# A spectral mix and a gated ReLU feed-forward on one core: the first pair's weights in a layout of their own, and v + g·z made ready in the second sequence round

## The chip, the cores and the metric

The kernel runs on one core of a Trainium2 chip. The metric is the device time of one execution in microseconds (us). The engines are TensorE (PE, matrix multiplication), VectorE (DVE, element-wise work from SBUF and PSUM), ScalarE (ACT, activations and casts), GpSimd (POOL) and SyncE (SP). Here POOL and SP only start transfers between the memory (HBM) and the on-chip memory (SBUF).

## The reference

With x of 2048 x 512, weights of 512 x 1792 (gate, up) and 1792 x 512 (down), and real and imaginary DFT matrices:

```python
g = _sigmoid((x * gate_w).sum(-1, keepdims=True))
a = x @ dft_hid_re.T ;  b = x @ dft_hid_im.T
y = dft_seq_re @ a - dft_seq_im @ b
v = (relu(x @ W_gate) * (x @ W_up)) @ W_down
return g * y + (1 - g) * v
```

(the einsums written as products). The result is v + g·(y − v).

## The kernel before

**Arithmetic.** Every float32 operand is split into a high part (a cast to the PE's float32 format, `h`) and a low part (the rest, `l`). A product is three matmuls: high·low, low·high and high·high (`PARTS`). The casts are made on ACT (`scalar.copy`), the low parts on DVE (`tensor_sub`). Around this lies a scheme of seven block products in place of eight (`LEFT`, `RIGHT`, `ORDER`), so many sums of blocks go through DVE. A matmul is 128 x 128 against 128 x 512.

**Stages, in PE's order.**

1. A warm-up of eight matmuls on a constant tile (`warm_up`).
2. The first pair of hidden blocks for the first half of the tokens, without the seven-product scheme (`Direct`, 96 matmuls). It uses the raw slots of the weights `w0` in the layout of all others, four slots by two halves of d. Slots 1 and 3 are loaded first, then 0 and 2, each as a strided load.
3. The other pairs (`Block`), gate and up, with ReLU and the product h = relu(gate)·up. h and its sums go to the memory (`hd`).
4. The DFT along the hidden axis (`SpectralBlock`), stored as `ad`, and the two last pairs.
5. Two rounds with the down weights (`Down`). They read `hd`, and write v to `vd` and −v to `zd`.
6. Four rounds of the DFT along the sequence (`Sequence(left, m, p)`), 336 matmuls or 76.2 us each. m is 0 for the real part, 1 for the imaginary part, p is the half of the columns of tokens. Their order is (0, 0), (0, 1), (1, 1), (1, 0). The rounds with m = 0 accumulate their result into `zd` by DMA, so that `zd` holds the real part of y minus v. The rounds with m = 1 take `zd` up, multiply by the gate g, add v and store `out`. So out = v + g·(z of this round + zd).

In a round the products come in the order 1, 3, 5, 7, 6, 2, 4. Blocks 12 and 22 are complete after product 6 (`done`), block 11 after product 2 (`middle`) and block 21 after product 4 (`end`). The DFT matrix is loaded as `r11`, `r22`, `r12`, `r21`, four tiles of each per round (`rights`), summed on DVE (`r<-r,r`), cast on ACT (`ch`) and split on DVE (`cl`). The left operands of the rounds with m = 1 are loaded from `lb` during the second round.

**What sets the order.** A planner in Python (`Plan`) collects every operation with a key, which is the place in PE's order near which it is wanted. `due` (lines 178 to 187) gives each a due time from its users, `order` (189 to 252) makes a list schedule with modelled times, a pool of 51 tiles in SBUF (4 KB for each partition) and eight PSUM banks. PE keeps program order, DVE and ACT take what is ready among the next 48 by due time, SP and POOL take transfers in the order of the plan. The chip then runs each engine's list in order, with semaphores. A load's place in SP's list is therefore fixed, and it waits for the tile it goes into to be free. Every instruction is issued in `Step.run`, so all have line L123 in the profile, and operations are told apart by their tiles.

**The places that the change touches.** `Step` and `Plan` (costs and due times), `x_load` (372), `Weights.load` (412), `block` (449), `Direct` (540 to 579), `Sequence` (847 to 920), `warm_up` (927) and the opening loads behind it, the loop over the rounds (1052 to 1057), and the layout of the inputs on the host (1093 to 1103). The opening loads, which SP issues in this order:

```python
(w0.load, 0, (1, 4, 2)), (x_load, 0, "11", (0, 1)), (x_load, 0, "11", (1, 2)), (w0.load, 1, (1, 4, 2)),
(x_load, 0, "21"), (lambda: load(gwt[:], gw),), (w0.load, 0, (0, 4, 2)), (w0.load, 1, (0, 4, 2)),
(w1.load, 0), (x_load, 0, "12"), (x_load, 0, "22"), (w1.load, 1)
```

Of the kernel before, what the change touches and what calls it, by code (L numbers as in the profile page):

```python
# [89 lines left out]
class Step:  # L90


    def __init__(self, key, engine, name, a, k):
# [13 lines left out]
        if name == "dma_start":  # L107
# [18 lines left out]
class Plan:  # L126
# [5 lines left out]


# [44 lines left out]
    def due(self):  # L178

        last, n = {}, self.now  # L180
        for s in reversed(self.steps):
            if s.engine == "tensor" and s.key >= 0:
                n -= 1
            mine = n if s.engine == "tensor" else s.key + self.REST
            s.due = min(mine * self.MATMUL, last.get(s, 1e9) - s.work - (self.LANDING if s.name == "dma_start" else 0))
            for x in s.after:
                last[x] = min(last.get(x, 1e9), s.due - self.WAIT)

    def order(self):
# [12 lines left out]
        while any(todo.values()):  # L202
            best = None
            for e, queue in todo.items():
                found = None
                for s in queue[:1 if e == "tensor" else 48]:
# [31 lines left out]
            if s.name == "dma_start":  # L238
                free[s.engine] = t + (0.9 if s.engine == "gpsimd" else 0.06)
# [39 lines left out]
def kernel(ctx: ExitStack, tc, xP, xG, wgu, wd, cr, ci, wri, gw, out):  # L279
# [77 lines left out]

    def store(o, i):
# [13 lines left out]
    def x_load(q, b, ks=(0, 2)):  # L372
        k, j = int(b[0]) - 1, int(b[1]) - 1
        ks = slice(*ks)
        load(piece[q, b][:, ks], xP[2 * q + j, k, :, ks])
# [28 lines left out]
    class Weights:  # L404
# [7 lines left out]
        def load(self, i, s=(0, 4, 1)):  # L412
            s = slice(*s)
            load(self.raw[i][:, s], wgu[self.c, i, :, s])
# [33 lines left out]

    def block(w, i, s):
        s = slice(s, 4, 2)  # L450
        E().scalar.copy(w.b[i][0][:, s], w.raw[i][:, s])
        E().vector.tensor_sub(w.b[i][1][:, s], w.raw[i][:, s], f32(w.b[i][0][:, s]))
# [87 lines left out]
    class Direct:  # L540
        def __init__(self, w):
            self.w, self.x = w, {b: [buf(f"xb{b}{x}", dtype=F32R) for x in "hl"] for b in ("11", "21", "12", "22")}
# [3 lines left out]
            for j in range(2):  # L546
                for d in range(2):
                    for i in range(2):
                        for f in range(2):
                            pe(6, self.product, d, f, i, j)  # L550
                            if d == 1:
                                op(plan.now, self.evac, f, i, j)
            h_out(0, w.c, self.h, plan.now + 200)

        def x_hi(self, b, ks=(0, 2)):
            ks = slice(*ks)
            E().scalar.copy(self.x[b][0][:, ks], piece[0, b][:, ks])

        def x_lo(self, b, ks=(0, 2)):
            ks = slice(*ks)  # L560
            E().vector.tensor_sub(self.x[b][1][:, ks], piece[0, b][:, ks], f32(self.x[b][0][:, ks]))

        def product(self, d, f, i, j):
            ps = self.ps[f, j]
            if d == 0 and i == 0:
                ps.new()
            x = self.x["12"[d] + "12"[j]]
            s = {(1, 1): 0, (0, 0): 1, (0, 1): 2, (1, 0): 3}[f, d]
            for k in range(2):
                for n, (a, b) in enumerate(reversed(PARTS)):  # L570
                    mm(ps[i], self.w.b[i][a][:, s, k], x[b][:, k], start=d == 0 and k == 0 and n == 0,
                       stop=d == 1 and k == 1 and n == 2)
# [274 lines left out]
    class Sequence(Round):  # L847
        HI, LO = 31, 24

        def __init__(self, left, m, p, last=False):  # L850
            self.m, self.p, self.last = m, p, last
# [19 lines left out]
        def gate(self, b):  # L871
            return self.g[:, int(b[1]) - 1].unsqueeze(1).to_broadcast([P, 2, N])

        def done(self, b, key):
# [7 lines left out]
            key += 42 if self.last else 62  # L882
            op(key, lambda: E().vector.tensor_mul(o.all, o.all, self.gate(b)))
            op(key + 2, lambda: E().vector.tensor_add(o.all, o.all, v.all))
            op(key + 8, lambda: load(out[self.place(b)], o.all))

        def middle(self, key):
            if not self.last:
                return super().middle(key)
            z, v = buf("z"), buf("v")  # L890
            op(key - 60, lambda: load(z.all, zd[self.place("11")]))
            op(key - 60, lambda: load(v.all, vd[self.place("11")]))

            def go():
                self.both(E().vector.tensor_add, z, self.ps["A"], z)
                E().vector.tensor_mul(z.all, z.all, self.gate("11"))
                E().vector.tensor_add(v.all, v.all, z.all)
                load(out[self.place("11")], v.all)
            op(key + 14, go)

        def end(self, key):
            if not self.last:
                return super().end(key)

            z, v, o = buf("z"), buf("v"), self.o["21"]
            t, _, es = self.place("21")
            op(key - 90, lambda: load(z.all, zd[t, :, es]))
            op(key - 90, lambda: load(v.all, vd[t, :, es]))

            def ahead():  # L910
                E().vector.tensor_sub(z.all, z.all, self.u2.all)
                E().vector.tensor_mul(z.all, z.all, self.gate("21"))
                E().vector.tensor_add(v.all, v.all, z.all)
            op(key - 32, ahead)
            for n in range(2):
                def go(n=n):
                    E().vector.tensor_mul(o[:, n], self.ps["D"][n], self.g[:, 0])
                    E().vector.tensor_sub(v[:, n], v[:, n], o[:, n])
                    load(out[t, :, es.start + n], v[:, n])
                op(key - 6 + 6 * n, go)  # L920
# [15 lines left out]
    w0, w1 = Weights(0), Weights(1)  # L936
# [3 lines left out]
    for f, *a in (  # L940
            (w0.load, 0, (1, 4, 2)), (x_load, 0, "11", (0, 1)), (x_load, 0, "11", (1, 2)), (w0.load, 1, (1, 4, 2)),
            (x_load, 0, "21"), (lambda: load(gwt[:], gw),), (w0.load, 0, (0, 4, 2)), (w0.load, 1, (0, 4, 2)),
            (w1.load, 0), (x_load, 0, "12"), (x_load, 0, "22"), (w1.load, 1)):
        op(-99, f, *a)
    direct = Direct(w0)
# [3 lines left out]
    op(-90, block, w0, 0, 1)  # L949
    for k in range(2):  # L950
        op(-90, direct.x_hi, "11", (k, k + 1))
        op(-90, direct.x_lo, "11", (k, k + 1))
    op(-90, block, w0, 1, 1)
    op(-90, direct.x_hi, "21")
    op(-90, direct.x_lo, "21")
    op(-90, block, w0, 0, 0)
    op(-90, block, w0, 1, 0)
    op(-90, w1.a_sum, 0)
    op(-90, w1.b_sum, 0)
    op(-90, direct.x_hi, "12")  # L960
    op(-90, w1.a_lo, 0)
# [149 lines left out]
```

## Time and profile before

| what | value |
|---|---|
| median of 3 runs | 798.02 us (798.01 to 798.16) |
| the profiled execution | 798.82 us, span 797.0 us |
| PE busy | 788.4 us (99%), 3464 matmuls |
| weight loads (PEld, beside PE) | 650.9 us (82%) |
| DVE busy | 660.3 us (83%), 784 instructions |
| ACT busy | 330.8 us (42%) |
| POOL busy | 89.4 us (11%) |
| moved by DMA | 188.07 MB, 236 GB/s over the span |

A row of the timeline gives the start in us, the duration, the engine, the operation, the tile written `<-` the tiles read, and how many instructions the row joins. In brackets stands the idle time of the engine before it and what ended it. `xb11h` is the high part of x's block 11, `wb0l` the low part of the first weight tile, `wr` the raw weights. The start of one matmul to the start of the next is shorter than its duration, since they are pipelined. The windows give for each stretch the busy time of every engine with its count of instructions, the granted clock of TensorE, the busy share of the 16 DMA engines and the GB/s. The view of waits names the tile whose writer ended an idle time of PE.

### The profile page before, as it was taken

The numbers are of one execution on the slowest core, as the hardware profiler recorded it, in microseconds if no ns is written. First come the engines' busy times: TensorE is split into PE (matmuls) and PEld (weight loads), VectorE is DVE, ScalarE is ACT, GpSimd is POOL, SyncE is SP. The second block draws the span as 40 slices with busy tenths as digits, with TensorE's granted clock in tenths as the row PEclk, the third lists the DMA queues.
The fourth block names the chain that finished last, engine by engine and source line by source line (L and its number), as shares of the span: only waits on it lengthen the run. The fifth ranks groups of instructions, "written<-read, shape, count | busy, mean of one in ns | idle before, by whom it ended". The sixth has DMA issues, their size and how long they took to land.

```text
span 797.0 us, 9541 instructions
## 1 busy us (share of the span) xinstructions
PE 788.4 (99%) x3464; PEld 650.9 (82%) x3464; DVE 660.3 (83%) x784; ACT 330.8 (42%) x394; POOL 89.4 (11%) x142
## 2 busy tenths in 40 slices
PE   8999999999999999999999999999999999999997
PEld 6888888888888888888888888888888888888885
DVE  6999977768699566899896799997697559977998
ACT  6533222212133134274666668463344235433440
POOL 0101311111112113111121001001000100010000
PEclk9999999999999999999999999999999999999999
DMA  8614553232547599999899989217877994198435
GB/s 321 246 41 145 179 205 146 92 146 93 197 146 228 203 341 417 409 357 330 298 369 415 408 301 346 103 54 196 286 275 272 273 382 135 42 278 314 177 114 158
DMA packets 54111, 188.07 MB, mean 236 GB/s; under 512 B 6192, under 2 KB 7216, under 8 KB 54064
## 3 DMA queue, kind: packets, MB, share of 16 engines
q1 hardware_dynamic: 35344, 119.30, 41.7%
q0 software_dynamic: 18720, 68.17, 24.5%
q8 instruction: 27, 0.44, 0.2%
q14 instruction: 20, 0.16, 0.1%
HBM read 118.23 MB, written 69.21 MB: 235 GB/s over the span
## 4 chain that ended last, share of the span: by engine, by line
PE 84%; DVE 7%; DMA 4%; issue 2%; ACT 1%; SPq 0%; POOLq 0%; ACTq 0%; POOL 0%; DVEq 0%
PE z L123 42%; PE c L123 32%; PE a L123 10%; DVE cl L123 2%; DVE z L123 2%; DVE r L123 2%; DMA r<-ci 2%; DMA z<-zd 1%; DMA wr<-wgu 1%; ACT ch L123 1%; SPq L123 0%; DVE v L123 0%; DVE w L123 0%; DVE xs L123 0%; DVE xb12l L123 0%
## 5 line engine op out<-in xcount | busy, mean ns | idle before, releaser
L123 ACT CAST ch<-r 128x1024 fp32r<-128x1024 f32 x112 | 115.8, 1052 | 131.1 <-PE z L123 53.3
L123 PE MATMUL z<-ch,ll 128*128 128x512 f32 x420 | 163.4, 389 | 0.0
L123 PE MATMUL z<-cl,lh 128*128 128x512 f32 x420 | 163.4, 389 | 0.0
L123 PE MATMUL z<-ch,lh 128*128 128x512 f32 x420 | 163.4, 389 | 0.0
L123 DVE TENSOR_TENSOR cl<-r,ch 128x1024 fp32r<-128x1024 f32 x112 | 134.5, 1220 | 29.1 <-ACT ch L123 22.9
L123 PE MATMUL z<-ch,lb 128*128 128x512 f32 x448 | 137.9, 389 | 0.0
L123 PEld LDWEIGHTS z<-ch,lb 128*128 128x128 f32 x448 | 84.1, 188 | 17.4
L123 PEld LDWEIGHTS z<-ch,lh 128*128 128x128 f32 x420 | 78.8, 188 | 16.5
L123 PEld LDWEIGHTS z<-cl,lh 128*128 128x128 f32 x420 | 78.8, 188 | 16.4
L123 PEld LDWEIGHTS z<-ch,ll 128*128 128x128 f32 x420 | 78.8, 188 | 16.2
L123 PE MATMUL z<-cl,lb 128*128 128x512 f32 x224 | 87.1, 389 | 0.0
L123 DVE TENSOR_TENSOR r<-r,r 128x1024 f32<-128x1024 f32 x64 | 76.4, 1218 | 3.5 <-DMA r<-cr 2.3
L123 DVE TENSOR_TENSOR cl<-hr,ch 128x1024 fp32r<-128x1024 f32 (+1 forms) x56 | 59.9, 1086 | 14.2 <-ACT ch L123 14.0
L123 ACT CAST ch<-hr 128x1024 fp32r<-128x1024 f32 (+1 forms) x56 | 51.8, 942 | 27.1 <-DMA hr<-hd 14.8
L123 PEld LDWEIGHTS z<-cl,lb 128*128 128x128 f32 x224 | 42.0, 188 | 8.8
L123 ACT ACTIVATE g<-c 128x512 f32<-128x512 f32 x26 | 15.6, 598 | 63.7 <-PE c L123 63.5
L123 PE MATMUL c<-xh,wb0l 128*128 128x512 f32 x104 | 40.5, 389 | 0.0
L123 PE MATMUL c<-xl,wb0h 128*128 128x512 f32 x104 | 40.5, 389 | 0.0
L123 PE MATMUL c<-xh,wb0h 128*128 128x512 f32 x104 | 40.5, 389 | 0.0
L123 PE MATMUL c<-xh,wb1l 128*128 128x512 f32 x104 | 40.5, 389 | 0.0
L123 PE MATMUL c<-xl,wb1h 128*128 128x512 f32 x104 | 40.5, 389 | 0.0
L123 PE MATMUL c<-xh,wb1h 128*128 128x512 f32 x104 | 40.5, 389 | 0.0
(210 smaller groups left out, 1318.6 us busy)
## 6 DMA issues: line engine op xcount, KB each, us to landing
hr<-hd SPq DMA_DIRECT2D x42, 512.0 KB, 7.1
r<-cr SPq DMA_DIRECT2D x32, 512.0 KB, 4.9
r<-ci SPq DMA_DIRECT2D x32, 512.0 KB, 11.9
hd<-hs POOLq DMA_DIRECT2D x28, 512.0 KB, 4.6
lb<-lb SPq DMA_DIRECT2D x28, 512.0 KB, 4.7
ad<-a POOLq DMA_DIRECT2D x16, 512.0 KB, 5.9
l<-ad SPq DMA_DIRECT2D x16, 512.0 KB, 8.6
wr<-wgu SPq DMA_DIRECT2D x14, 512.0 KB, 6.4
```

The source lines that it names most:

```text
L123: getattr(getattr(nc, self.engine), self.name)(*map(ap, self.a), **{k: ap(x) for k, x in self.k.items()})
```

## The change

Three things are changed.

*The first pair.* Its weights come as an input of their own, `wf`, with d outermost: for each of two tiles of d, 128 partitions by two halves k by four column groups. A half is one load of 256 KB, 2 KB in one piece for each partition. SP issues the four halves, and ACT's queue issues the four halves of x's blocks 11 and 21 (`side`). The weights `w0` are then loaded in the shared layout only for the later stage. The 48 products for the first tokens run with d, k and the part n outermost, so that four matmuls follow on one part; the high half of x11 is cast on DVE, the others on ACT. The warm-up tile is filled by one memset without a cast. The loads of x12 and x22 come ahead of those of `w1`, and `gwt` last; the sums of `w1` and x get keys in place of a written order.

*The planner.* It gets a cost for `tensor_copy`, 0.5 us for the issue of a transfer in place of 0.06, another rule for due times, and beside the next 48 operations the oldest one as a candidate.

*The last rounds.* The last round's class is now `Last`. Its `prepare` puts work into the second round: the gate row, loads of the four blocks of `zd` and `vd` for p = 0, v + g·z on DVE (8 operations), and four stores into `vd` from POOL. In the last round z of this round is multiplied by g, and v comes as an accumulating transfer (blocks 12 and 22) or as a load, with the sum made by halves (blocks 11 and 21).

```diff
+        if name == "tensor_copy":
+            self.work = 0.1 + n * 0.52e-3
+            self.hold = self.work - 0.05
...
+    ISSUE = {"sync": 0.5, "scalar": 0.5, "gpsimd": 0.9}
...
-            mine = n if s.engine == "tensor" else s.key + self.REST
-            s.due = min(mine * self.MATMUL, last.get(s, 1e9) - s.work - (self.LANDING if s.name == "dma_start" else 0))
+            if s.engine == "tensor":
+                last[s] = min(last.get(s, 1e9), n * self.MATMUL)
+            elif s not in last or s.key > 0:
+                last[s] = min(last.get(s, 1e9), (s.key + self.REST) * self.MATMUL)
+            s.due = last[s] - (s.work + self.LANDING if s.name == "dma_start" else 0)
             for x in s.after:
-                last[x] = min(last.get(x, 1e9), s.due - self.WAIT)
+                last[x] = min(last.get(x, 1e9), s.due - self.WAIT - (x.work if x.name != "dma_start" else 0))
...
-                for s in queue[:1 if e == "tensor" else 48]:
+                near = queue[:1] if e == "tensor" or not queue else [*queue[:48], min(queue, key=turn.get)]
+                for s in near:
...
-                free[s.engine] = t + (0.9 if s.engine == "gpsimd" else 0.06)
+                free[s.engine] = t + self.ISSUE[s.engine]
...
+    def side(o, i):
+        plan.scalar.dma_start(o, i)
...
+            for d in range(2):
+                for k in range(2):
+                    for n in range(3):
+                        for i in range(2):
+                            pe(2, self.products, [(d, i, f, 0, k, n) for f in range(2)])
...
+        def w_split(self, d, k=slice(0, 2)):
+            hi, lo = self.w[d]
+            E().scalar.copy(hi[:, k], self.raw[d][:, k])
+            E().vector.tensor_sub(lo[:, k], self.raw[d][:, k], f32(hi[:, k]))
+
+        def x_split(self, b, k=slice(0, 2), hi=None):
+            x, raw = self.x[b], piece[0, b]
+            (hi or E().scalar.copy)(x[0][:, k], raw[:, k])
+            E().vector.tensor_sub(x[1][:, k], raw[:, k], f32(x[0][:, k]))
...
+    class Last(Sequence):
+        def prepare(self, key):
+            g = gate_row(self.p, key - 60)
+            for i, b in enumerate(BLOCKS):
+                k, z, v = key + 24 * i, buf("z"), buf("v")
+                op(k - 50, lambda b=b, z=z: load(z.all, zd[self.place(b)]))
+                op(k - 50, lambda b=b, v=v: load(v.all, vd[self.place(b)]))
+                op(k, lambda b=b, z=z: E().vector.tensor_mul(z.all, z.all, self.gate(b, g)))
+                op(k + 2, lambda v=v, z=z: combine(v.all, v.all, z.all, 1))
+                op(k + 10, lambda b=b, v=v: store(vd[self.place(b)], v.all))
+
+        def done(self, b, key):
+            o = self.o[b]
             op(key, lambda: E().vector.tensor_mul(o.all, o.all, self.gate(b)))
-            op(key + 2, lambda: E().vector.tensor_add(o.all, o.all, v.all))
-            op(key + 8, lambda: load(out[self.place(b)], o.all))
+            op(key + 4, lambda: accumulate(o.all, vd[self.place(b)]))
+            op(key + 30, lambda: load(out[self.place(b)], o.all))
+
+        def part(self, v, b, n, p, sign):
+            E().vector.tensor_mul(self.o[b][:, n], p[n], self.g[:, 0])
+            combine(v[:, n], v[:, n], self.o[b][:, n], sign)
...
-            z, v, o = buf("z"), buf("v"), self.o["21"]
+            v = buf("v")
             t, _, es = self.place("21")
-            op(key - 90, lambda: load(z.all, zd[t, :, es]))
-            op(key - 90, lambda: load(v.all, vd[t, :, es]))
...
-    ones, warm, wp = buf("ones", [N]), buf("warm", [N], F32R), Pair("warm")
+    warm, wp = buf("warm", [N], F32R), Pair("warm")
 
     def warm_up():
-        E().vector.memset(ones.all, 1.0)
+        E().vector.memset(f32(warm.all), 1.0)
         E().vector.memset(gs.all, 0.0)
-        E().vector.tensor_copy(warm.all, ones.all)
...
+    for d, b in ((0, "11"), (1, "21")):
+        for k in halves:
+            op(-99, direct.w_load, d, k)
+            op(-99, x_load, 0, b, k, side)
+    for f, *a in ((x_load, 0, "12"), (x_load, 0, "22"), (w1.load, 0), (w1.load, 1), (lambda: load(gwt[:], gw),)):
+        op(-98, f, *a)
...
+    for d, b in ((0, "11"), (1, "21")):
+        for k in halves:
+            op(-90, direct.x_split, b, k, plan.vector.tensor_copy if d == 0 else None)
+            op(-90, direct.w_split, d, k)
...
         if n == 1:
+            start = plan.now
...
-        Sequence(lefts[m], m, p, n == 3)
+        if n < 3:
+            Sequence(lefts[m], m, p)
+        else:
+            Last(lefts[m], m, p).prepare(start + 150)
...
+    first = wgu[0][:, :, [[1, 3], [2, 0]]].transpose(2, 1, 4, 0, 3, 5).reshape(2, P, 2, 4, P)
```

More of the change, by code (lines that the diff above doesn't have):

```diff
@@ L278, with kernel @@
 @with_exitstack
-def kernel(ctx: ExitStack, tc, xP, xG, wgu, wd, cr, ci, wri, gw, out):
+def kernel(ctx: ExitStack, tc, xP, xG, wf, wgu, wd, cr, ci, wri, gw, out):
     nc = tc.nc
@@ L559, in x_lo @@
[L559 to L572, printed above, removed]
+            for d in range(2):
[3 more added lines that the diff above has]
+                            pe(2, self.products, [(d, i, f, 0, k, n) for f in range(2)])
+                            if d == k == 1 and n == 2:
+                                for f in range(2):
+                                    op(plan.now, self.evac, f, i, 0)
@@ L881, in done @@
             op(key + 20, lambda: load(v.all, vd[self.place(b)]))
-            key += 42 if self.last else 62
-            op(key, lambda: E().vector.tensor_mul(o.all, o.all, self.gate(b)))
-            op(key + 2, lambda: E().vector.tensor_add(o.all, o.all, v.all))
-            op(key + 8, lambda: load(out[self.place(b)], o.all))
-        def middle(self, key):
[L888 to L899, printed above, removed]
+            op(key + 62, lambda: E().vector.tensor_mul(o.all, o.all, self.gate(b)))
@@ L914, in end @@
-            op(key - 32, ahead)
+                E().vector.tensor_mul(self.u2.all, self.u2.all, self.gate("21"))
+                combine(v.all, v.all, self.u2.all, -1)
+            op(key - 90, lambda: load(v.all, vd[self.place("21")]))
+            op(key - 40, ahead)
             for n in range(2):
[L916 to L920, printed above, removed]
+                op(key - 6 + 6 * n, self.part, v, "21", n, self.ps["D"], -1)
+                op(key - 6 + 6 * n, lambda n=n: load(out[t, :, es.start + n], v[:, n]))
@@ L1096 @@
         "xG": laid(x.reshape(NT, KD, P, D).transpose(0, 2, 1, 3)),
-        "wgu": laid(np.stack([blocks(wg), blocks(wu)], axis=1)),
+        "wf": laid(first),
+        "wgu": laid(wgu),
         "wd": laid(halves(wd)),
```

117 lines of the change are left out of this document (48 added, 69 removed).

## The prediction, made before the result was known

> **What bounds the kernel now.** I read the page's first part, then what TensorE (PE) waited for, then the span cut where PE's work changes character, then the single instructions at both ends.
>
> ```profile
> PE 788.4 (99%) x3464; PEld 650.9 (82%) x3464; DVE 660.3 (83%) x784; ACT 330.8 (42%) x394; POOL 89.4 (11%) x142
> ```
> ```profile
> PE warm L123 <- DVE warm L123: 1.9, 1, 1.9
> PE c L123 <- DVE xb11l L123: 0.5, 2, 0.2
> PE c L123 <- DVE xb12l L123: 0.3, 1, 0.3
> PE c L123 <- ACT xb11h L123: 0.3, 1, 0.3
> ```
> ```profile
> 0.00:5.49 5.49, 3.57 (x8) 2.51 (x8) 1.66 (x5) 2.52 (x3) 0.20 (x4) 1.00 0.51 156
> 5.49:18.79 13.30, 12.27 (x50) 9.04 (x50) 10.54 (x15) 8.45 (x11) 1.28 (x2) 1.00 1.02 381
> 18.79:791.40 772.61, 772.55 (x3407) 639.37 (x3407) 646.10 (x763) 319.83 (x381) 87.95 (x136) 1.00 0.66 234
> 791.40:797.00 5.60, 0.00 (x0) 0.00 (x0) 2.00 (x4) 0.00 (x0) 0.00 (x0) 0.71 0.48 187
> ```
>
> PE is busy 99% of the span, and its list of waits has nothing but the first stage. From 18.79 to 791.40 us it is idle 0.06 us in all. So nothing can be won between these times unless matmuls go, and none goes. What can be won lies before 18.79 and behind PE's last matmul; what can be lost lies anywhere. The rate is 772.61 / 3407 = 0.2268 us per matmul.
>
> The sum is made against the profiled execution, 798.82 us (a span of 797.0 and 1.8 around it). The median of the runs shown is 798.02, 0.8 lower; I carry the difference over. About 0.2%, or 1.6 us, is what a measurement of this kernel can tell from no change.
>
> **The front.** The window 5.49 to 18.79 holds 49 products besides the last warm-up matmul. At 0.2268 each they need 11.11 us and take 13.30: 2.19 us are lost there.
>
> ```profile
> 1.92 3.64 PE L123 MATMUL warm<-warm 128*128 128x512 f32 x8 [1.92 <-DVE warm L123]
> 5.49 0.49 PE L123 MATMUL c<-xb11h,wb0h 128*128 128x512 f32 x1
> 6.22 0.50 PE L123 MATMUL c<-xb11l,wb0h 128*128 128x512 f32 x1 [0.23 <-DVE xb11l L123]
> 18.79 0.50 PE L123 MATMUL c<-xb12l,wb0h 128*128 128x512 f32 x1 [0.32 <-DVE xb12l L123]
> ```
> ```profile
> 0.73 1.28 ACT L123 ACT_TABLE_LOAD   x1 [0.73 <-PEq L1104]
> 3.92 0.62 ACT L123 CAST wb0h<-wr 128x512 fp32r<-128x512 f32 x1 [1.90 <-DMA wr<-wgu]
> 4.82 0.62 ACT L123 CAST xb11h<-x 128x512 fp32r<-128x512 f32 x1 [0.29 <-DMA x<-xP]
> 6.54 0.62 ACT L123 CAST xb11h<-x 128x512 fp32r<-128x512 f32 x1 [1.10 <-DMA x<-xP]
> 7.90 0.62 ACT L123 CAST wb1h<-wr 128x512 fp32r<-128x512 f32 x1 [0.74 <-DMA wr<-wgu]
> ```
> ```profile
> 1.43 0.43 DVE L123 CAST warm<-ones 128x512 fp32r<-128x512 f32 x1
> 5.47 0.69 DVE L123 TENSOR_TENSOR xb11l<-x,xb11h 128x512 fp32r<-128x512 f32 x1 [0.21 <-ACT xb11h L123]
> ```
> ```profile
> 0.74 0.66 SPq L123 DMA_DIRECT2D wr<-wgu  x1
> ```
> ```profile
> GB/s 0 0 0 0 51 322 395 272 221 234 223 211 227 250 311 367 402 371 344 389 422 444 418 401 401 434 401 418 418 401 401 434 401 410 401 410 418 401 401 434
> ```
>
> The pieces of 256 KB set the pace: ACT's casts start as they land, at 3.92 (weights), 4.82 and 6.54 (the halves of x) and 7.90 (weights). In slices of 0.5 us the DMA rate falls from 395 to 211-234 GB/s between 3.5 and 7 us, while the odd slots of w0 move in pieces of 1 KB, and later stands above 400.
>
> *First product.* The new weights come in halves of 2 KB pieces, so the two first pieces (512 KB) should move at about 400 GB/s rather than 220: before, 520 KB had moved by 4.0 and the second piece was in use at 4.82. I put the landing at 4.5, between 3.9 (where the first piece alone was in use) and 5.3 (both late by the lag of the second). ACT now issues four loads first, four times up to 0.66 as on SP from 0.73, then loads its table, 1.28: free at up to 4.65. Its cast takes 0.62, hand-over 0.05. First product: 5.3 to 5.4; I take 5.4. Below, the warm-up sets the end: without the CAST it begins 0.43 earlier and ends near 5.06. Above, 6.0.
>
> *The 49 products.* x11's high part is now a cast on DVE (0.43, as the CAST row) beside ACT's cast of the weights, and four products share each part. For a landing L, DVE does x high to L+0.43, x low (0.69) to about L+1.1, weights low to L+1.75; PE wants them at L+1.6 and L+2.5. The second half is wanted at L+3.4; before, the fourth piece was in use 3.08 behind the second, and 0.62 for its cast makes L+3.7. So 0.15 is lost there (0 to 0.9), where the waits of 0.2 to 0.3 in PE's list, each with a slow restart behind it (6.22 is 0.73 behind 5.49), made most of the 2.19. The warm-up's eight matmuls take 3.64, 0.45 each, half the later rate; up to four first products could run so if the change of rate is late: 4 x 0.2 = 0.8 at most, I take 0.2. x12 comes before the c=1 weights now, so the wait at 18.79 (0.32 by its row) goes. Losses 0.35 instead of 2.19.
>
> The Trainium skill (TensorE: Matmul & The Clock Gate, What's actually happening) says that the array runs at half rate until one busy window of about 3.4 us, which is free-running. The trace agrees for this start (the warm-up is slow from 1.92 to 5.49, 3.6 us); by that rule the 0.2 can be anything up to the 0.8.
>
> The front thus ends (5.49 - 5.4) + (2.19 - 0.35) = 1.9 us earlier. All behind it follows, PE in the same order. The planner's new costs move little on the other engines; the nearest place is a block in which DVE now makes three additions of hs ahead of a product h<-g,c that PE's bank waits for.
>
> ```profile
> 346.15 0.68 DVE L123 TENSOR_TENSOR h<-g,c 128x512 f32<-128x512 f32 x1
> 346.74 0.69 DVE L123 TENSOR_TENSOR hs<-h 128x512 f32<-128x512 f32 x1
> 349.18 0.39 PE L123 MATMUL c<-xh,wb1l 128*128 128x512 f32 x1
> ```
>
> The evacuation ends at 346.83, PE uses the bank at 349.18: 2.35 us of slack, of which three additions, 0.61 from one start to the next, take 1.8. I cost this at nothing; without that cover it would be 1.8.
>
> **The tail.**
>
> ```profile
> 790.95 0.39 PE L123 MATMUL z<-ch,lb 128*128 128x512 f32 x1
> 791.45 0.69 DVE L123 TENSOR_TENSOR v<-v,z 128x512 f32<-128x512 f32 x1
> 792.06 0.68 DVE L123 TENSOR_TENSOR z<-z,gg 128x512 f32<-128x512 f32 x1
> 792.77 0.69 DVE L123 TENSOR_TENSOR v<-v,z 128x512 f32<-128x512 f32 x1
> 792.17 1.66 SPq L123 DMA_DIRECT2D out<-v  x2
> ```
>
> The last matmul ends at 791.34; the last multiplication starts only at 792.06 because DVE is still at the subtraction of the half before it (791.45). In the new order the additions of v for blocks 12 and 22 are gone from DVE (POOL adds by DMA, earlier), so DVE is idle when each half of the last product comes: the first half's pair fits into the time of the second half's matmuls, the last multiplication starts at 791.37. 792.06 - 791.37 = 0.69 off; the subtraction (0.69), its store's issue and landing follow unchanged.
>
> **The second round.** Here the new work goes: 1 gate row, 4 loads of z, 4 of v, 8 DVE operations, 4 stores on POOL.
>
> ```profile
> 581.00:602.00 21.00, 21.00 (x94) 17.38 (x94) 19.15 (x18) 10.48 (x12) 0.00 (x0) 1.00 0.84 300
> 602.00:622.00 20.00, 20.00 (x90) 16.57 (x89) 14.75 (x16) 7.29 (x7) 0.00 (x0) 1.00 0.74 252
> 622.00:640.00 18.00, 18.00 (x82) 14.88 (x81) 8.94 (x9) 5.18 (x6) 2.55 (x3) 1.00 0.99 277
> 640.00:659.00 19.00, 19.00 (x85) 15.76 (x84) 10.68 (x10) 6.86 (x8) 0.84 (x1) 1.00 0.96 359
> ```
> ```profile
> lb<-lb SPq DMA_DIRECT2D x16, 512.0 KB, 4.1
> GB/s 233 198 229 254 323 267 259 272 259 254 285 263 280 272 272 272 280 375 410 427 418 418 418 427 414 414 405 293 276 272 267 418 414 418 418 423 418 194 17 267
> r<-ci SPq DMA_DIRECT2D x10, 512.0 KB, 12.7
> ```
> ```profile
> 657.24 2.35 DVE L123 TENSOR_TENSOR r<-r,r 128x1024 f32<-128x1024 f32 x2
> 659.66 2.36 DVE L123 TENSOR_TENSOR cl<-r,ch 128x1024 fp32r<-128x1024 f32 x2
> ```
> ```profile
> 663.56 0.39 PE L123 MATMUL z<-cl,lb 128*128 128x512 f32 x1
> ```
>
> DVE: 8 operations of 1.18 (the pair at 657.24), 9.4 us, against 41 - 33.9 = 7.1 us idle from 581 to 622. DVE works several us ahead of PE there and is idle for about half of 622 to 659, so they delay its later work by 2.3 and stop nothing; without that lead it would be the 2.3. The first of them waits for the gate row and for z, which SP issues near 581 and 584, 4.1 us before they land as the loads there do; DVE comes to it near 591, and what is queued behind it, the low parts for the next product, is wanted at 598. POOL is idle from 581 to 622, so its four stores hold up nothing.
>
> DMA: 13 transfers of 512 KB are 6.8 MB; at the 414-418 GB/s of full slices, 16.4 us. By bytes, 581 to 622 moved 6.3 + 5.0 = 11.3 MB of a possible 17.0: 13.7 us are spare. By the busy shares only 0.16 x 21 + 0.26 x 20 = 8.6. So 2.7 to 7.8 us are still queued at 622. From there to 659 the queues are full (0.99, 0.96) and take up 0.9 more; the third round's loads, which wait 12.7 us from issue to landing already, land 1.8 to 6.9 later. The nearest need: r's sum at 657.24, the low part at 659.66 (one of the two, ends 660.88), its product at 663.56: 2.68 us of slack. Stall: 0 to 4.2. Full slices move at the high rate, so the count by bytes is nearer; I take a delay of 3.2 and a stall of 0.5. In the last round two z and two v loads go, which can't move PE: it has no wait there.
>
> **Sum**: -1.9 - 0.7 + 0.5 = -2.1. Profiled execution 796.7, median 795.9.
>
> **The rivals.** *(B) The front's gain stays out.* ACT's issues and table load last to 4.65, and both queues share the same engines; if the pieces land as they did (4.82, 7.90), first product 5.5, restart 0.9, half rate 0.8: losses 1.7, front -0.5, sum -0.7, median 797.3. For it: the slices up to 3.5 us show that the first bytes come no earlier than 2 us. Against: the 220 GB/s belong to the 1 KB pieces. The Trainium skill (DMA: Bandwidth & Descriptors, Issuing engines are not separate DMA queues) says that loads started on different engines interleave on the same 16 engines and save only issue time. No run here shows two queues at the start yet; if it holds, the second queue is worth only the 0.7 of an issue, as I have it.
>
> *(C) The queue eats it.* Delay 5 to 6.9, stall 2.3 to 4.2, sum -0.3 to +1.6: median 797.7 to 799.6, the middle 798.5. For it: the busy share, which leaves 8.6 us only.
>
> *(D) Slower.* The same queue, if it takes in nothing of the load: with SP's loads in order, a backlog over 7.8 us makes the stall over 4.2 and the time over 799.6. With all 16.4 us behind (less 0.9 and 2.68: 12.8) it would be 808. Against: the slices show room.
>
> *(E) Better:* no stall, first product at 5.1, loss 0.1: -2.5 - 0.7 = -3.2, median 794.8.
>
> **How the numbers follow.** A with its own range (795.0 to 796.6): 0.46; E 0.14; B 0.14; C 0.13; D 0.13. Faster by over 0.2% (below 796.4): E, and A but for a small part, 0.57. Same: B, C and the rest of A, 0.30. Slower: D, 0.13. The likeliest is A, 795.9. The range leaves out D, and half of C: 794.5 to 798.4.
>
> **What would show it.** Of the changed kernel: the first product starts at 5.1 to 5.6 and the 49th ends near 16.9 (B: 18 and later). PE's list of waits shows waits for cl or ch of r in the third round of 0.5 us in all; 2 or more means C, more than 4 D. The median from issue to landing of r<-ci rises from 12.7 to about 15. The last multiplication follows the last matmul within 0.1 us. The prediction is wrong if the second queue delays ACT's table load beyond 4.7, if the reordered additions stall a block, or if SP, which issues in order, holds r's loads behind a z load that waits for its accumulation.

## The result, and the profile after

The changed kernel takes 800.73 us (median of 9, 799.47 to 801.66) against 798.3 for the kernel before (median of 9, 798.01 to 799.08): a ratio of 1.0029, interval 1.0018 to 1.0039. It is slower, by about 2.4 us; the prediction was 795.9 with a range of 794.5 to 798.4. The profiled execution took 801.54 us, with a span of 799.7, 2.7 us over the span of before. One execution of a run below, at 1140.92 us with a mean granted clock of 0.655, belongs to a slow state of the chip and counts in no ratio.

The page's first part and PE's list of waits, of the changed kernel:

```profile
span 799.7 us, 9573 instructions
PE 790.3 (99%) x3464; PEld 652.1 (82%) x3464; DVE 665.6 (83%) x791; ACT 329.1 (41%) x393; POOL 91.7 (11%) x146
```
```profile
PE warm L126 <- DVE gs L126: 1.5, 1, 1.5
PE z L126 <- DVE cl L126: 1.3, 2, 0.8
PE z L126 <- ACT ch L126: 0.7, 1, 0.7
PE c L126 <- ACT wf0h L126: 0.6, 1, 0.6
```

Two lines are new: PE waits in a sequence round (`z`) for a low part and a high part of r. The windows, cut at the new first product and around these waits (busy time with count, clock, DMA share, GB/s):

```profile
5.85:18.82 12.97, 12.97 (x50) 10.59 (x50) 12.66 (x20) 7.62 (x11) 0.71 (x1) 1.00 1.04 407
18.82:604.00 585.18, 585.18 (x2583) 484.58 (x2582) 491.00 (x618) 245.81 (x303) 80.72 (x128) 1.00 0.67 243
640.00:670.00 30.00, 27.89 (x120) 21.88 (x119) 18.98 (x17) 12.29 (x13) 0.84 (x1) 1.00 0.85 319
670.00:793.60 123.60, 123.60 (x547) 102.36 (x546) 110.55 (x104) 48.16 (x51) 5.07 (x6) 1.00 0.52 166
```

From 18.82 to 604 and from 670 on PE never waits. From 640 to 670 it is idle for 2.1 us; with the slow restarts (the first start after a wait is followed by the next after 0.34 us instead of 0.23) the matmuls come 3.2 us later than they would. And the front, though PE was busy in all of 5.85 to 18.82, ends where it ended before: the fiftieth product starts at 18.82, against 18.79. Why shows in the products themselves:

```profile
1.45 3.78 PE L126 MATMUL warm<-warm 128*128 128x512 f32 x8 [1.45 <-DVE gs L126]
5.85 2.05 PE L126 MATMUL c<-xb11h,wf0h 128*128 128x512 f32 x4 [0.62 <-ACT wf0h L126]
7.69 1.91 PE L126 MATMUL c<-xb11l,wf0h 128*128 128x512 f32 x4
9.40 1.17 PE L126 MATMUL c<-xb11h,wf0l 128*128 128x512 f32 x4
10.41 1.09 PE L126 MATMUL c<-xb11h,wf0h 128*128 128x512 f32 x4
```
```profile
5.10 0.62 ACT L126 CAST wf0h<-wf 128x512 fp32r<-128x512 f32 x1 [1.20 <-DMA wf<-wf]
```
```profile
5.28 0.43 DVE L126 CAST xb11h<-x 128x512 fp32r<-128x512 f32 x1 [3.84 <-DMA x<-xP]
```

Eight products from 5.85 to 9.40 take 0.44 us each, the rate of the warm-up; from 10.41 four take 0.93. No restart is left, but 49 x 0.2268 = 11.11 take 12.97: 1.86 us are lost to the half rate alone. The clock column of the window reads 1.00 all the same: the trace's record of the granted clock begins only with the full clock, at 9.57 us here and at 5.26 in the kernel before, so at the start the rate is read from the starts of the matmuls. The pieces came at 5.1 (weights) and 5.3 (x), not at 4.5. In slices of 0.25 us the start of the DMA traffic, the changed kernel first, then the kernel before:

```profile
GB/s 0 0 0 0 0 0 8 106 197 238 319 188 229 180 139 213 336 401 410 410 393 361 369 377 352 377 393 434 401 418 410 385 295 377 393 410 426 475 344 426
```
```profile
GB/s 0 0 0 0 0 0 0 0 41 61 262 381 406 385 283 262 205 238 262 205 209 238 180 242 234 221 213 287 242 381 397 336 410 393 381 360 348 340 373 406
```

With pieces of 2 KB alone the rate is 140 to 320 GB/s from 2 to 3.75 us, no better than what I had put down to the pieces of 1 KB; before, with those pieces among the first, it reached 406.

The third round, at the first of its stalls: ACT and PE of the changed kernel, then the cast for the same tile before.

```profile
652.12 1.05 ACT L126 CAST ch<-r 128x1024 fp32r<-128x1024 f32 x1 [5.22 <-DMA r<-ci]
```
```profile
653.22 0.50 PE L126 MATMUL z<-ch,lb 128*128 128x512 f32 x1 [0.71 <-ACT ch L126]
654.48 0.50 PE L126 MATMUL z<-cl,lb 128*128 128x512 f32 x1 [0.76 <-DVE cl L126]
```
```profile
644.26 1.05 ACT L123 CAST ch<-r 128x1024 fp32r<-128x1024 f32 x1 [2.75 <-PE z L123]
```

The second tile of r22 is cast as it lands: at 652.12, 7.9 us later than before; PE stands at 653.22 and 654.48. The next stalls, at 663 and 666, are those of r12. The delay is there when SP issues the load, which is the sixth load of r for this round (the first of the two in each row; the changed kernel first):

```profile
636.95 3.20 SPq L126 DMA_DIRECT2D r<-ci  x2
628.63 2.59 SPq L123 DMA_DIRECT2D r<-ci  x2
```

It is issued 8.3 us later, while the median from issue to landing rises from 12.7 only to 13.4. SP's loads use eight semaphores in turn, and by the landings of the trace each load from 626.95 to 648.59 is issued within 0.1 us behind the landing of the eighth load before it (this one at 636.95, behind 636.89). So what stands ahead in SP's list holds up what is wanted next. The windows over the two rounds show the traffic behind it:

```profile
581.00:602.00 21.00, 21.00 (x94) 17.41 (x93) 18.13 (x17) 7.86 (x9) 0.56 (x1) 1.00 0.96 342
602.00:622.00 20.00, 20.00 (x90) 16.54 (x89) 17.07 (x16) 8.13 (x8) 1.62 (x3) 1.00 1.01 401
622.00:640.00 18.00, 18.00 (x81) 14.92 (x80) 13.93 (x15) 5.23 (x7) 2.57 (x3) 1.00 1.05 335
640.00:659.00 19.00, 17.53 (x77) 13.94 (x76) 8.07 (x8) 7.01 (x8) 0.84 (x1) 1.00 1.03 383
```

The engines are full from 581 to 659, at 335 to 401 GB/s; before, they had been at 0.84 and 0.74 of the time in the first two windows.

The tail, of the changed kernel:

```profile
794.12 0.39 PE L126 MATMUL z<-ch,lb 128*128 128x512 f32 x1
```
```profile
794.55 0.69 DVE L126 TENSOR_TENSOR z<-z,gg 128x512 f32<-128x512 f32 x1
795.27 0.69 DVE L126 TENSOR_TENSOR v<-v,z 128x512 f32<-128x512 f32 x1
```

The last multiplication starts 0.04 us behind the last matmul's end (794.51), where it had been 0.72. The balance against the profiled execution of before: front +0.03, stalls +3.2, tail -0.7, the last stores +0.2: +2.7, the difference of the spans.

### The profile page after: what moved, and what is told of

The parts are those of the page before. It is cut to its first block, busy times and chain, and to the rows that moved or that the text cites. A ratio compares the mean times of both kernels' runs of the same rounds, so it can differ in the third digit from the quotient of the medians.

```text
span 799.7 us, 9573 instructions
## 1 busy us (share of the span) xinstructions
PE 790.3 (99%) x3464; PEld 652.1 (82%) x3464; DVE 665.6 (83%) x791; ACT 329.1 (41%) x393; POOL 91.7 (11%) x146
## 3 DMA queue, kind: packets, MB, share of 16 engines
q10 hardware_dynamic: 576, 1.05, 0.4%
## 4 chain that ended last, share of the span: by engine, by line
PE 91%; DMA 6%; DVE 2%; ACT 0%; issue 0%; SPq 0%; ACTq 0%; DVEq 0%
PE z L126 48%; PE c L126 34%; PE a L126 10%; DMA r<-ci 4%; DMA lb<-lb 1%; DVE cl L126 1%; DMA wf<-wf 1%; DVE r L126 0%; ACT ch L126 0%; DVE v L126 0%; DVE z L126 0%; ACT wf0h L126 0%; SPq L126 0%; ACTq L126 0%; DVEq L126 0%
## 5 line engine op out<-in xcount | busy, mean ns | idle before, releaser
L126 DVE TENSOR_TENSOR cl<-hr,ch 128x1024 fp32r<-128x1024 f32 (+1 forms) x56 | 59.9, 1087 | 13.4 <-ACT ch L126 10.8
```

The source lines that it names most:

```text
L126: getattr(getattr(nc, self.engine), self.name)(*map(ap, self.a), **{k: ap(x) for k, x in self.k.items()})
```

## The experiments

The runs were made in three groups, on one chip and beside runs of the kernel before; differences are to the group's median of before (799.03 for the first four runs, 798.5 for the next four, 798.63 for the last three). An edit changes what the planner sorts, so the order on the other engines can shift with it.

**Ten warm-up matmuls.** Theory: the pause between warm-up and first product spoils the start of the full clock.

```diff
-    WARM = 8
+    WARM = 10
```

> The changed kernel with ten warm-up matmuls in place of eight, which cover the 0.62 us between the warm-up's end (5.23) and the first product (5.85). Theory of the clock: the half rate of the first products (5.85 to 9.40 for eight of them, 1.7 us lost) comes of that gap, which spoils the stretch in which PE would have earned the full rate; then the first product still starts near 5.85, the products run at 0.227 at most 1 us later, and the time falls by 0.8 to 1.7 us against the changed kernel (800.73 to about 799.3). Rival, the start of the full rate has nothing to do with the gap: eight slow products again, no change within 0.3 us. Second rival, the warm-up only delays the first product: 0.3 us slower.

800.32 us, ratio 1.0018 (1.0009 to 1.0027), +1.3: in the ratio 0.9 us under the changed kernel, the low end of what the theory allowed. In the profiled execution the 49 products lose 0.18 us instead of 1.86. But with 802.23 it is the longest, and shows two things more (the last row is a window, with the granted clock in its third place from the end):

```profile
PE z L126 <- DVE cl L126: 2.8, 4, 1.9
```
```profile
612.22 0.50 PE L126 MATMUL z<-cl,lh 128*128 128x512 f32 x1 [1.93 <-DVE cl L126]
613.72 0.57 PE L126 MATMUL z<-cl,lh 128*128 128x512 f32 x1
```
```profile
613.80:617.10 3.30, 3.30 (x10) 2.54 (x9) 3.30 (x4) 1.70 (x3) 0.00 (x0) 0.50 1.02 416
```

PE stands for 1.93 us in the second round, at a place where the changed kernel's profiled execution did not wait, and shortly after runs eight matmuls at about half rate (613.72 to 617.08), with a granted clock of 0.50. By the starts of the matmuls the two cost 3.8 us; stalls of the third round take another 1.7. Eight of the eleven executions lie between 799.77 and 800.45 and three from 801.4; which of them had the half rate is not seen in their times.

**The old last round.** The class `Sequence` with its flag `last`, its `middle` and `end`, as before; front and planner new. Of the edit, the loop over the rounds:

```diff
-        if n < 3:
-            Sequence(lefts[m], m, p)
-        else:
-            Last(lefts[m], m, p).prepare(start + 150)
+        Sequence(lefts[m], m, p, n == 3)
```

> The changed kernel with the last round as before (no work put into the second round); new front and new planner stay. Theory of the queue: the stall of 3.2 us in the third round (waits for cl and ch at 652 to 667) comes of the 13 added transfers; it goes, the tail's 0.5 to 0.7 comes back, so the time falls by 2.5 to 2.7 against the changed kernel, to about 798.1, level with the kernel before. Rival, the planner's other order makes the stall: it stays, and the time rises to about 801.3.

796.54 us, ratio 0.9966 (0.9954 to 0.9979): 2.5 below the kernel before, where I had expected it level. PE waits for nothing behind the warm-up's tile and the first product's weights:

```profile
PE c L126 <- ACT wf0h L126: 0.6, 1, 0.6
```
```profile
789.30 0.69 DVE L126 TENSOR_TENSOR z<-z,gg 128x512 f32<-128x512 f32 x1
```

The stalls belong to the new last round. The front's gain is there too: the five executions lie between 796.0 and 796.89, and in the profiled one the fiftieth product starts at 16.85. And the last multiplication follows the last matmul (788.87 + 0.39) at once, so the tail's gain does not need the new last round.

**The new last round alone,** on the old front and the old planner. Of the edit, the loop:

```diff
-        Sequence(lefts[m], m, p, n == 3)
+        if n < 3:
+            Sequence(lefts[m], m, p)
+        else:
+            Last(lefts[m], m, p).prepare(start + 150)
```

> The kernel before with the change of the last rounds alone (old front, old planner). Theory of the queue: a stall of about 3 us in the third round, -0.5 to -0.7 at the tail, the time 2 to 3 us over the kernel before, 800.3 to 801.2. Rival, the planner's order is needed for the stall: 797.6 to 798.0, faster by 0.3 to 0.7.

801.95 us, ratio 1.0039 (1.0025 to 1.0053), +2.9, as the theory of the queue has it, with the stalls in the third round (at 653, 662 and 665) and one of 0.8 us at 425 besides, in the first `Down` round, where the run with the planner alone has one of 0.4; what makes it I did not find out.

```profile
PE z L123 <- DVE cl L123: 2.2, 3, 1.5
```
```profile
794.72 0.69 DVE L123 TENSOR_TENSOR z<-z,gg 128x512 f32<-128x512 f32 x1
```

Its last matmul ends at 794.68 (794.29 + 0.39), and the last multiplication follows 0.04 later: under the old planner too, the new last round gives the tail's gain.

**Later loads of two left operands.**

```diff
-                    lefts[1].fetch(x, k, plan.now + 48 * i + 24 * k + 40, lb)
+                    lefts[1].fetch(x, k, plan.now + 48 * i + 24 * k + (40 if i < 5 else 200), lb)
```

> The changed kernel with the loads of the left operands for products 2 and 4 (8 transfers of 512 KB, wanted at 693 to 713 us) keyed 160 matmuls later, behind the jam instead of in it; the added work stays in the second round. Theory of the queue: r22 and r12 of the third round no longer stand behind these 10 us of transfers, the stall of 3.2 us goes, the time falls to 797.3 to 797.8, below the kernel before. Rival, the eight added operations on DVE make the stall: the waits stay and the time is 800.5 to 800.9.

796.82 us, ratio 0.9976 (0.9963 to 0.9989), -2.2. The stalls of 652 to 667 are gone with the eight DVE operations still there. In the profiled execution (798.44, one of the two longest of ten; eight are at 797.31 or below) a stall is left in the second round, and its DVE rows say how it comes about:

```profile
601.98 1.22 DVE L126 TENSOR_TENSOR cl<-r,ch 128x1024 fp32r<-128x1024 f32 x1
606.69 1.23 DVE L126 TENSOR_TENSOR z<-z,gg 128x1024 f32<-128x1024 f32 x1 [3.49 <-DMA z<-zd]
609.45 1.23 DVE L126 TENSOR_TENSOR v<-v,z 128x1024 f32<-128x1024 f32 x1 [1.54 <-DMA v<-vd]
610.59 2.35 DVE L126 TENSOR_TENSOR cl<-r,ch 128x1024 fp32r<-128x1024 f32 x2
```
```profile
611.86 0.50 PE L126 MATMUL z<-cl,lh 128*128 128x512 f32 x1 [1.85 <-DVE cl L126]
```
```profile
594.84 14.52 DMA v<-vd
```

DVE stands 3.49 us for the third z and 1.54 for its v, which took 14.52 us from issue to landing. The low part for PE's next product, ready to be made, stands behind them in DVE's order; PE waits 1.85.

**The transfers without DVE's work.**

```diff
-                op(k, lambda b=b, z=z: E().vector.tensor_mul(z.all, z.all, self.gate(b, g)))
-                op(k + 2, lambda v=v, z=z: combine(v.all, v.all, z.all, 1))
```

> The changed kernel with the added loads and stores of the second round, but without the eight DVE operations (v is stored back as it was loaded, so v + g z is left out for half of the columns). Theory of the queue: SP's loads still stand behind the 13 transfers, so the stalls of the third round (waits for cl or ch between 652 and 667) stay, 2 to 3.3 us; the wait at 610 to 612, where DVE stood in order behind a sum that waited for v, goes. Time 0 to 1 us below the changed kernel. Rival, DVE's added work makes the stalls: PE waits for nothing after the front, time 797 to 798.

799.93 us, ratio 1.0018 (1.0009 to 1.0028), +1.4. The stalls of the third round are all there, 3.3 us with their restarts, and there is none at 610.

```profile
PE z L126 <- DVE cl L126: 1.5, 3, 0.8
PE z L126 <- ACT ch L126: 0.8, 1, 0.8
```

**DVE's work without the transfers.** The eight operations run on the gate row, nothing is loaded or stored for them.

```diff
-                op(k - 50, lambda b=b, z=z: load(z.all, zd[self.place(b)]))
-                op(k - 50, lambda b=b, v=v: load(v.all, vd[self.place(b)]))
-                op(k, lambda b=b, z=z: E().vector.tensor_mul(z.all, z.all, self.gate(b, g)))
-                op(k + 2, lambda v=v, z=z: combine(v.all, v.all, z.all, 1))
-                op(k + 10, lambda b=b, v=v: store(vd[self.place(b)], v.all))
+                op(k, lambda b=b, z=z: E().vector.tensor_mul(z.all, self.gate(b, g), self.gate(b, g)))
+                op(k + 2, lambda v=v, z=z: combine(v.all, z.all, z.all, 1))
```

> The changed kernel with the eight DVE operations, on the gate row instead of z and v, and without the added loads of z and v and the stores (v + g z is left out). Theory of the queue: no stall in the second and third round, time 796 to 797.5. Rival, DVE's work makes the stalls: 2 to 3 us of waits for cl stay, time near 800.

Ratio 0.9987 (0.9973 to 1.0000). Nine of the ten executions fall into two groups, 796.2 to 796.9 (five) and 798.8 to 799.2 (four); their median, 796.88, lies in the expected span (with the tenth, of 1140.92, it would be 797.83). The profile is that of the tenth execution, so its waits are not read. The lower group is level with the old last round: there DVE's work alone cost nothing. What makes the upper group was not seen; a pause ahead of the first product, below, makes one of this kind.

**The new planner alone,** on the kernel before: the lines of `Step` and `Plan` in the diff of the change.

```diff
+    ISSUE = {"sync": 0.5, "scalar": 0.5, "gpsimd": 0.9}
```

> The kernel before with the new planner's costs and due times alone. From the run with the old last round, where the last multiplication already followed PE at once, I expect the tail's 0.5 to 0.7 us from the planner and nothing else: 0.5 to 0.7 below the kernel before. Rival, the tail's gain needs another part of the change: level with the kernel before within 0.2.

797.81 us against 798.5, -0.7, but the interval of the ratio (0.9985 to 1.0004) takes in no change. The profile shows the tail's gain:

```profile
790.84 0.39 PE L126 MATMUL z<-ch,lb 128*128 128x512 f32 x1
```
```profile
791.26 0.69 DVE L126 TENSOR_TENSOR z<-z,gg 128x512 f32<-128x512 f32 x1
```

The last multiplication starts 0.03 behind the last matmul's end. So the planner is enough for it, as the old last round with the new planner showed already; the new last round under the old planner is enough too.

**One queue at the start.**

```diff
-            op(-99, x_load, 0, b, k, side)
+            op(-99, x_load, 0, b, k)
```

> The changed kernel with the halves of x issued on SP, between the weights, in place of ACT's queue. Two queues share the engines: the two first pieces land at 5.1 and 5.3 with two queues; if the interleaving costs, they land earlier with one, as the kernel before had (3.9 and 4.8), and the first product starts at 5.1 to 5.5 instead of 5.5 to 5.9. Rival, the second queue helps by the issue times: the second piece lands 0.7 later and the first product starts at 6.2 or later. The time of the whole differs by less than 0.7 either way, because the stalls of the second and third round stay.

800.89 us, ratio 1.0042 (1.0026 to 1.0058), +2.4. The expectation fell: the first x is cast at 6.12, and the first product starts at 6.70, where the profiled executions with two queues have 5.5 to 5.9.

```profile
6.70 2.04 PE L126 MATMUL c<-xb11h,wf0h 128*128 128x512 f32 x4 [1.46 <-DVE xb11h L126]
```
```profile
6.12 0.43 DVE L126 CAST xb11h<-x 128x512 fp32r<-128x512 f32 x1 [4.68 <-DMA x<-xP]
```
```profile
3.42 0.62 ACT L126 CAST wf0h<-wf 128x512 fp32r<-128x512 f32 x1 [1.40 <-DMA wf<-wf]
```

With one queue the weights, issued first, are in use at 3.42, 1.7 us earlier than with two (5.10), and x, issued second, at 6.12, 0.84 later; SP issued x only 0.45 us later (1.18 against 0.73). The product needs both and so started later. But this is one profile, of the longest of seven executions (804.98), and the kernel before, with one queue too, had its x in use at 4.82. What the second queue is worth is not settled by it. The time of the whole is level with the changed kernel's by the medians (+2.4 in both), and 1.0 us longer by the ratios (1.0042 against 1.0029); up to 0.7 was expected. The profile has the stall of the second round too:

```profile
614.86 0.50 PE L126 MATMUL z<-cl,lh 128*128 128x512 f32 x1 [1.76 <-DVE cl L126]
```

**Old last round, ten and six warm-up matmuls.** Two runs that differ in the number of warm-up matmuls, and so in the pause: the edit of the old last round, and

```diff
-    WARM = 8
+    WARM = 10
```

or `WARM = 6`.

> The run with the old last round (new front, new planner) and ten warm-up matmuls, so that PE has no pause ahead of the first product. Theory of the clock: the slow first products (up to 1.8 us lost, in some executions and not in others) come of that pause; with it closed no execution has them, the times lie within 0.6 us of each other but for single ones, and the median is 0.3 below to 0.2 above that of eight warm-up matmuls (796.54, all of whose executions were of the quick kind), that is 2.2 to 2.8 under the kernel before. Rival, the pause has nothing to do with it: a second group of times 1.5 to 2 us higher remains.

> The same with six warm-up matmuls, so that the pause ahead of the first product grows by 0.85 to about 1.4 us. Theory of the clock: more executions, or all, have eight or more products at half rate; median 1 to 2 us over the run with ten. Rival, the pause doesn't matter and the full rate comes a fixed time after the first matmul: no difference beyond 0.3.

Ten: 796.53 us, ratio 0.9971 (0.9962 to 0.9981), all ten executions between 796.07 and 796.94. Six: 797.72, ratio 0.9982 (0.9972 to 0.9992), and two groups, five executions at 796.19 to 796.68 and seven at 797.64 to 798.53. The profiled one, of the upper group:

```profile
1.45 2.93 PE L126 MATMUL warm<-warm 128*128 128x512 f32 x6 [1.45 <-DVE gs L126]
5.70 2.05 PE L126 MATMUL c<-xb11h,wf0h 128*128 128x512 f32 x4 [1.32 <-DVE xb11h L126]
7.55 1.91 PE L126 MATMUL c<-xb11l,wf0h 128*128 128x512 f32 x4
9.25 1.35 PE L126 MATMUL c<-xb11h,wf0l 128*128 128x512 f32 x4
```

After a pause of 1.32 us eight products run at half rate, as in the changed kernel after 0.62. With ten there is no pause, though the profiled execution still has three slow products (0.66 us lost, against 2.04 with six):

```profile
5.88 1.69 PE L126 MATMUL c<-xb11h,wf0h 128*128 128x512 f32 x4
```

With the pause closed the upper group is gone. These two runs change the length of the warm-up as well, but the traces' record of the granted clock sets the pause apart. Counted from the first warm-up matmul, the full clock came after 3.1 to 5.9 us in the six profiled executions without a pause (eight or ten warm-ups), after 3.3 to 5.3 us in the three with pauses of 0.31 to 0.55, and after 8.1, 8.3 and 9.6 us in the three with pauses of 0.62 (the changed kernel, eight warm-ups), 1.32 (six) and 1.46 (one queue, eight). So the late starts stand behind pauses of 0.6 us or more, and eight warm-up matmuls are in all three sets. Without a pause some products can be slow as well: the kernel before had the full clock after 3.3 us, the run with the new last round alone, whose front is the same, after 5.9.

**The new last round with the loads spread.** Ten warm-up matmuls, and four left operands fetched later.

```diff
-    WARM = 8
+    WARM = 10
...
-                    lefts[1].fetch(x, k, plan.now + 48 * i + 24 * k + 40, lb)
+                    lefts[1].fetch(x, k, plan.now + (40, 88, 136, 250, 300, 440, 488)[i] + 24 * k, lb)
```

> The changed kernel (new last round) with ten warm-up matmuls and the loads of the left operands for products 7, 6, 2 and 4 of the third round keyed 66 to 160 matmuls later, so that fewer of them stand in SP's queue between the added loads and ahead of r22 and r12. Theory of the queue: DVE no longer waits 2 to 3 us for z and v near 605, the stalls at 610 and at 652 to 667 go or fall under 0.5 us in all, and the time is level with the run with the old last round and ten warm-up matmuls, within 0.5. Rival, the new last round costs by DVE's work itself: 1 us or more above it.

796.93 us, ratio 0.9974 (0.9965 to 0.9982), 0.4 above the old last round with ten warm-ups: within the 0.5 of the theory. PE waits for nothing but the warm-up's tile:

```profile
PE warm L126 <- DVE gs L126: 1.5, 1, 1.5
```

## Why the prediction was wrong, step by step

*The front, -1.9 expected.* The mechanism was right: x12's wait and the restarts are gone. In the profiled execution the gain was 0.0, because the term for the half rate was mis-sized: 0.2, at most 0.8 for four products, against 1.86 for eight. I had taken the bound from one execution in which no pause was; the warm-up, which now begins and ends earlier, and the later pieces (5.1 and 5.3 against 4.5) together opened one of 0.6. The Trainium skill (TensorE: Matmul & The Clock Gate, What's actually happening) has the full rate follow one busy window of about 3.4 us that runs freely; the trace agrees, with 3.55 us at half rate behind the pause, in some executions and not in others. I quoted that rule, and let it change only the size within my bound. Where the pause is closed or does no harm, the gain is there: the old last round is 2.5 below the kernel before, of which I estimate 1.8 for the front, the planner alone having 0.7 (2.5 - 0.7); its fiftieth product starts 1.94 us earlier.

*The landing at 4.5* was wrong by 0.6 to 0.8, because the low rate of the first microseconds is not that of 1 KB pieces alone. What it is stays open. ACT was no limit: its table load ended at 3.90 (2.62 + 1.28), not 4.65. I had the second queue save the issue time alone; whether it saves more stays open too.

*The tail, -0.7*, was right in size (0.68), and its mechanism holds: with the new last round alone, under the old planner, DVE is idle when the last half comes and the multiplication follows 0.04 behind the last matmul. What I did not see is that the new planner gives the same without it (0.03), so that the work moved into the second round bought nothing that the planner's part of the change did not already have.

*The second round, +0.5 expected.* This is the step that failed and decides. The 13 transfers were counted rightly. But I let the later loads land 3.2 us later, in bounds of 1.8 to 6.9, and the tile of r22 landed 7.9 later, beyond them; the stall was 3.2 in place of 0.5, inside my range of 0 to 4.2. Two things were wrong. I chose the count by bytes over the busy share because full slices move 414 GB/s; the changed kernel's windows have the engines at 0.96 to 1.05 with 335 to 401 GB/s, so a share of 0.84 at 300 GB/s had 16% left, not 28%. The count by the share, with 7.8 us still queued, comes close. And I looked for the nearest need at the wrong tile: r12, with 2.68 of slack, and not r22, whose load stands in SP's list behind the backlog; both stalled.

*DVE* I followed for the first of the four pairs only, with 4.1 us from issue to landing for z, where the medians became 9.0 for z and 10.2 for v. It is the third pair that waits for its loads, with the low part for PE behind it. The two runs that take the halves apart agree: the transfers without the operations keep the third round's stalls and have none at 610, the operations without the transfers have a group of executions at 796.2 to 796.9.

*The signs.* The first product started at 5.85 (5.1 to 5.6 was the sign for A), the fiftieth at 18.82 (B), and PE waited 2.0 us for cl or ch of r (C). The r loads took 13.4 from issue to landing and not 15: the delay was in SP's list. The last multiplication followed within 0.1 us as said. So C's stall and B's slow front came together. Each had been priced with the other term as hoped, and no rival had both, so the median (800.73) went beyond them, to where only D stood.

The stall at 610 is a case apart. It came in the profiled executions of three runs (1.93, 1.85 and 1.76 us: ten warm-ups, later loads of two operands, one queue), and not in those of the changed kernel or of the new last round alone. The front's end does not decide it: two of the three had an early front (17.17 and 16.90 for the fiftieth product), the third the latest of all (19.98). What does stays open.

## What to carry to other kernels

In this kernel, spare DMA time had to be read from the busy share of the engines and not from bytes at the best rate over a whole round, and loads that are wanted 50 to 70 us later must not stand in the same in-order list ahead of those wanted next. Moving them turned a loss into a gain: the same work that cost 3.8 us (1.0018 against 0.9971, both with ten warm-ups) cost 0.2 to 0.4 with the loads spread. The warm-up has to last until the first real product; its length is set by the landing of the first pieces. And work moved off a critical end is worth testing against the cheapest rival: here the planner's new costs and due times gave the same tail without it. The lowest medians are those of the old last round with the new front and the new planner, 796.54 us with eight warm-up matmuls and 796.53 with ten.

## What the runs showed of the hardware

A pause of 1.93 us in the middle of the kernel, at the full clock since 6.19 us, was followed 1.5 us behind the restart by 3.4 us at a granted clock of 0.50 (the run with ten warm-ups, eight matmuls from 613.72 to 617.08). Pauses of 1.85 and 1.76 us at the same place in two other runs were not (the full clock stands through 605 to 625 us there), nor the waits of 0.7 and 0.8 us in the changed kernel (653.22, 654.48). A stall of that length thus cost nearly twice its own time in one execution of three. At the start the full clock came 3.1 to 5.9 us behind the first matmul where PE did not pause, and 8.1 to 9.6 us behind it where PE paused for 0.62 us or more (3.3 to 5.3 with pauses of 0.31 to 0.55). With one queue the first piece was in use 1.7 us earlier and the second 0.84 us later than with two, in one profile of each.
